# A gated mix of attention and a state-space convolution, rewritten around a list schedule

## The chip, the cores and the metric

The kernel runs on one core of a Trainium2 chip. Its time is the device time of one execution in microseconds (us). Three runs of the kernel before took 1487.04, 1490.69 and 1493.61 us; the median, 1490.69, is what the prediction is compared with. A core has five engines with an instruction stream each, which execute in order and meet at semaphores: PE (matmuls; PEld is its loading of weights), DVE (element-wise work), ACT (exponentials and other functions), POOL, and SP, which here only issues transfers. SBUF is the memory beside the engines; PSUM, with eight banks of 512 f32 columns on 128 partitions, is where matmuls write.

## The reference

```python
x = A_x                                        # 2048 positions x 448 channels, bf16
g = sigmoid((x * gate_w).sum(-1, keepdims=True))
# a: attention, 16 heads of 28, one shared key and value head
q = (x @ wq).reshape(1, 2048, 16, 28).transpose(0, 2, 1, 3); k = x @ wk; v = x @ wv
p = softmax(einsum("bhqd,bkd->bhqk", q, k) * 28 ** -0.5)
a = einsum("bhqk,bkd->bhqd", p, v).transpose(0, 2, 1, 3).reshape(1, 2048, 448) @ wo
# b: each channel d is convolved with its own causal kernel of 2048 lags, 256 complex modes n
logdA = exp(log_dt)[:, None] * (A_re + 1j * A_im); dB = exp(log_dt)[:, None] * (B_re + 1j * B_im)
K = einsum("dn,dnl,dn->dl", C_re + 1j * C_im, exp(logdA[:, :, None] * arange(2048)), dB).real
y = causal_convolution(x, K)                   # written there with FFTs of 4096
b = y + x * Dskip
out = g * a + (1 - g) * b
```

Each mode's power z^l is needed at 2048 lags l = 64 a + b. It is split into a power of z^64 (32 of them, called P, with the factor C dB) and a power of z below 64 (64 of them, Q), so that the kernel of a channel is a product of two small matrices over the modes.

## The kernel before

Everything is written out in an order fixed by hand: a list of instructions for each engine, with a wait wherever a result of another engine (or of DVE itself) is used. Phases follow each other: constants; x loaded and transposed (L297); weights; parameters of the convolution; keys, values and all sixteen query projections (L440), each with a bound on the scores (L452) taken from PSUM by ACT and DVE in turn; the gate; a copy of x by channel, U (L836); then the main phase, and an epilogue after a barrier over all engines.

**Attention, in the main phase.** 512 units go over 4 head groups g, 4 query chunks of 512, 16 key tiles of 128 and 2 pairs of heads. `emit_A` issues the two score matmuls of a unit (L520; 29 rows of the contraction each, so that two heads lie in different quarters of the array) into two of psA's four banks, and the exponential over both on ACT (L527, 1024 columns). `emit_B` issues the two matmuls with the values (L543) into psB0. PE runs two units ahead. At the end of each group of 32 units DVE copies the sums out (L552), PE spreads the row sums (L555), DVE takes the reciprocal of all 128 x 512 (L559) and multiplies (L562).

**The convolution, pumped between the units.** After each unit a step or two of two generators is issued.

- `gen_masters` and `gen_tables`: for a chunk of 16 channels (28 chunks) DVE squares z ten times, 32 columns an instruction (L909 to L926), and doubles the tables Q and P step by step, real and imaginary parts apart (L980 to L1001). Two chunks are interleaved.
- `gen_round`: 112 rounds, one for each group of 4 channels, and at first one for each chunk. A round may transpose the output of the round before (L1047) and copy it to Ysd (L1094), generates the kernels of a chunk (L1064: 64 matmuls of 64 columns; copied out at L1105 and written to the DRAM array KP_scratch by four transfers), and convolves a group (L1082: 17 blocks of 128 lags x 4 channels, 128 columns each; copied out at L1115). Rounds alternate between the banks psC0 and psC1.
- `gen_bts_dma`: the convolution multiplies by a matrix with constant diagonals, BtS, which is read from KP_scratch with rows that overlap: 4 x 2176 elements on each of 128 partitions, 2176 KB a group, two buffers.

All transfers of the main phase stand in SP's queue, in order.

**Epilogue.** 16 blocks of 128 positions: four matmuls with Wo (L642) and five DVE instructions (L653 to L666).

What sets the order is the pump, the same for every unit:

```python
for u in range(n_units):
    emit_unit(u)
    pump(ts, "ts_done", tab_quota)       # table steps: DVE
    if u >= 8:
        pump(rsi, "rs_done", rnd_quota)  # steps of rounds: PE, then DVE
```

## Time and profile before

| | us |
|---|---|
| runs | 1487.04, 1490.69, 1493.61 |
| profiled execution, span | 1487.7 |
| ACT busy, of it exponentials (L527) | 564.8, 518.5 |
| DVE busy | 844.6 |
| PE busy: scores L520, values L543, convolution L1082, kernel generation L1064 | 851.8: 276.0, 284.5, 223.5, 39.0 |
| largest DMA issue: BtS, 112 of 2176 KB, issue to landing (median) | 9.8 |

The profile is that of one execution. A group is the set of instructions of one line, engine and shape; behind the bar stand the group's busy time, the mean length of one in ns, and the idle time of the engine just before them with what ended it. A slice row gives, for 40 equal parts of the span, the busy share in tenths, and PEclk the clock that was granted to PE, in tenths of full speed (where it shows 9 before 222 us it has no record yet). Instructions of one engine may overlap a little, so busy time is less than count times length.

### The profile page before, as it was taken

The page shows a single profiled execution, that of the slowest core. Times are in us where ns is not written, and L with a number is a line of the kernel's source. Part 1 is how long each engine was busy: PE and PEld are TensorE (multiplying, and loading weights), DVE is VectorE, ACT ScalarE, POOL GpSimd, SP SyncE. Part 2 cuts the span into 40 slices and gives each one's busy share as a digit, 9 for nine tenths or more (in the row PEclk, how much of TensorE's full clock was granted, in tenths as well). Part 3 has the DMA queues.
Part 4 walks back from the last instruction along what each step waited for, and adds up shares of the span by engine and source line. Part 5 has one row for each costly group of instructions (what it writes and reads, how often), then busy time and mean ns, then how long its engine had stood idle before and what let it go on. Part 6 is the DMA issues. An engine that isn't in the chain of part 4 may idle for free.

```text
span 1487.7 us, 29922 instructions
## 1 busy us (share of the span) xinstructions
PE 851.8 (57%) x12049; PEld 342.3 (23%) x12049; DVE 844.6 (57%) x4331; ACT 564.8 (38%) x613; POOL 14.7 (1%) x24
## 2 busy tenths in 40 slices
PE   4276195445745467445746366656567665567644
PEld 2022111111212022111212133323233332223311
DVE  1522999999999999999999520200101001010058
ACT  4222084335634455435534333333333333333300
POOL 3000000000000000000000000000000000000000
PEclk9999998556665566656666656565566656665655
DMA  4000002213330233303331489989899898999922
GB/s 98 17 7 0 0 1 65 63 62 125 125 124 21 104 125 125 95 31 124 125 125 60 175 322 353 348 326 361 319 353 334 334 357 306 351 335 338 347 85 65
DMA packets 87355, 261.59 MB, mean 176 GB/s; under 512 B 20496, under 2 KB 29648, under 8 KB 87216
## 3 DMA queue, kind: packets, MB, share of 16 engines
q1 hardware_dynamic: 86464, 258.75, 48.8%
q0 software_dynamic: 752, 0.93, 0.4%
q8 instruction: 94, 1.54, 0.4%
q14 instruction: 45, 0.37, 0.1%
HBM read 255.77 MB, written 3.90 MB: 175 GB/s over the span
## 4 chain that ended last, share of the span: by engine, by line
DVE 47%; DMA 28%; PE 20%; issue 2%; ACT 1%; SPq 0%; DVEq 0%
DMA BtS<-KP_scratch 26%; PE psC L1082 8%; DVE tabQ L987 5%; DVE rden_sb L559 3%; PE psA L520 3%; PE psB L543 3%; DVE tmpT L984 3%; DVE tabQ L980 3%; DVE tabQ L981 3%; DVE U L836 2%; PE psA L440 2%; DVE mst L909 2%; DVE tmpT L983 2%; DVE tabP L994 2%; DVE tabP L993 2%
## 5 line engine op out<-in xcount | busy, mean ns | idle before, releaser
L527 ACT ACTIVATE expT<-psA 128x1024 bf16<-128x1024 f32 x512 | 518.5, 1024 | 760.8 <-PE psA L520 714.3
L1082 PE MATMUL psC<-BtS,U 128*16 128x128 bf16 x7616 | 223.5, 284 | 183.8 <-DMA BtS<-KP_scratch 183.5
L543 PE MATMUL psB<-expT,vaug 128*32 128x512 bf16 x1024 | 284.5, 552 | 48.4 <-DVE rden_sb L559 31.7
L520 PE MATMUL psA<-qT,kT 29*128 29x512 bf16 x1024 | 276.0, 536 | 5.0 <-DVE psC L1163 5.0
L1115 DVE CAST cstg<-psC 128x128 bf16<-128x128 f32 x112 | 32.3, 288 | 429.2 <-PE psC L1082 420.8
L1082 PEld LDWEIGHTS psC<-BtS,U 128*16 128x16 bf16 x7616 | 161.0, 115 | 257.0 <-DMA BtS<-KP_scratch 200.5
L1064 PE MATMUL psC<-tabQ,tabP 128*32 128x64 bf16 x1792 | 39.0, 241 | 159.1 <-DVE tabP L1001 159.1
L520 PEld LDWEIGHTS psA<-qT,kT 29*128 29x128 bf16 x1024 | 51.3, 97 | 212.7 <-issue 207.5
L543 PEld LDWEIGHTS psB<-expT,vaug 128*32 128x32 bf16 x1024 | 61.3, 115 | 148.2 <-ACT expT L527 107.5
L987 DVE TENSOR_TENSOR tabQ<-tabQ,tmpT 128x1024 bf16<-128x1024 bf16 (+2 forms) x168 | 75.8, 488 | 0.0
L1064 PEld LDWEIGHTS psC<-tabQ,tabP 128*32 128x32 bf16 x1792 | 29.5, 120 | 173.1 <-DVE tabP L1001 162.3
L559 DVE RECIPROCAL rden_sb<-psB 128x512 f32<-128x512 f32 x16 | 53.7, 3358 | 9.9 <-PE psB L555 9.9
L1094 DVE COPY Ysd<-psC 128x64 bf16<-128x64 bf16 x112 | 24.8, 222 | 50.1 <-PE psC L1047 50.1
L981 DVE TENSOR_TENSOR tabQ<-tabQ,mbf 128x512 bf16<-128x512 bf16 (+2 forms) x168 | 53.2, 317 | 0.0
L980 DVE TENSOR_TENSOR tabQ<-tabQ,mbf 128x512 bf16<-128x512 bf16 (+2 forms) x168 | 53.2, 317 | 0.0
L984 DVE TENSOR_TENSOR tmpT<-tabQ,mbf 128x512 bf16<-128x512 bf16 (+2 forms) x168 | 53.1, 316 | 0.0
L983 DVE TENSOR_TENSOR tmpT<-tabQ,mbf 128x512 bf16<-128x512 bf16 (+2 forms) x168 | 53.1, 316 | 0.0
L555 PE MATMUL psB<-acc_sb,cbf 128*128 128x512 bf16 x16 | 8.4, 526 | 74.3 <-DVE acc_sb L552 74.3
L909 DVE TENSOR_TENSOR mst<-mst 128x32 f32<-128x32 f32 x280 | 49.7, 178 | 0.0
L910 DVE TENSOR_TENSOR mst<-mst 128x32 f32<-128x32 f32 x280 | 49.7, 177 | 0.0
L1047 PE MATMUL psC<-cbf,cstg 128*128 128x128 bf16 x112 | 29.6, 264 | 35.0 <-DVE cstg L1115 35.0
L924 DVE CAST mbf<-mst 128x32 bf16<-128x32 f32 x280 | 47.0, 168 | 0.0
(123 smaller groups left out, 805.6 us busy)
## 6 DMA issues: line engine op xcount, KB each, us to landing
BtS<-KP_scratch SPq DMA_DIRECT2D x112, 2176.0 KB, 9.8
xstage<-in_A_x_dram SPq DMA_DIRECT2D x16, 112.0 KB, 2.1
KP_scratch<-kstg SPq DMA_DIRECT2D x112, 16.0 KB, 1.9
xs_epi<-in_A_x_dram SPq DMA_DIRECT2D x16, 112.0 KB, 2.0
out_dram<-osb SPq DMA_DIRECT2D x16, 112.0 KB, 1.7
Wo<-in_A_wo_dram POOLq DMA_DIRECT2D x4, 98.0 KB, 2.6
Wq<-in_A_wq_dram POOLq DMA_DIRECT2D x3, 112.0 KB, 4.8
xstage<-in_B_A_re_dram SPq DMA_DIRECT2D x3, 64.0 KB, 3.1
```

The costliest lines, as they stand in the source:

```text
L520: hsc = pg.op("pe", lambda e, hsl=hsl, kt=kt, g=g, qc=qc, slot=slot, hs2=hs2: e.matmul(psA.v(0, P, 1024 * slot + 512 * hs2, [[1, 512]]), k ...
L527: hact = pg.op("act", lambda e, slot=slot, es=es: e.activation(expT.v(0, P, es * 1024, [[1, 1024]]), psA.v(0, P, 1024 * slot, [[1, 1024]]) ...
L543: hpv = pg.op("pe", lambda e, hsl=hsl, kt=kt, es=es, hs2=hs2: e.matmul(psB0.v(32 * hsl, 32, 0, [[1, 512]]), vaug.v(0, P, 32 * kt, [[1, 32] ...
L559: h3 = pg.op("dve", lambda e: e.reciprocal(rden.v(0, P, 0, [[1, 512]]), psB0.v(0, P, 0, [[1, 512]])))
L909: h1 = pg.op("dve", lambda e, nre=nre, a=a: e.tensor_tensor(nre, a, a, ALU.mult))
L980: h1 = pg.op("dve", lambda e: e.tensor_tensor(q_c(0, b_dst, w), q_c(0, b_src, w), m_b(lvl, 0, w), ALU.mult))
L981: h2 = pg.op("dve", lambda e: e.tensor_tensor(q_c(1, b_dst, w), q_c(1, b_src, w), m_b(lvl, 0, w), ALU.mult))
L983: h3 = pg.op("dve", lambda e: e.tensor_tensor(tmp_c(0, w), q_c(1, b_src, w), m_b(lvl, 1, w), ALU.mult))
L984: h4 = pg.op("dve", lambda e: e.tensor_tensor(tmp_c(1, w), q_c(0, b_src, w), m_b(lvl, 2, w), ALU.mult))
L987: h5 = pg.op("dve", lambda e: e.tensor_tensor(q_both(b_dst, w), q_both(b_dst, w), tmp_both(w), ALU.add))
L1064: h_pe_last = pg.op("pe", lambda e, psC=psC, j=j, bl=bl, comp=comp, g8=g8, Q=Q, Pt=Pt, ci=ci: e.matmul(psC.v(32 * j, 32, 256 + 64 * bl, [[ ...
L1082: h_pe_last = pg.op("pe", lambda e, psC=psC, m=m, cg=cg, d=d, BtS=BtS: e.matmul(psC.v(32 * cg, 16, 0, [[1, 128]]), U.v(0, P, d * 32 + 16 - ...
```

## The change

The kernel is written anew. What it computes is the same; the parts are these.

1. **Order.** Operations are recorded with what they read and write, an estimated duration and a priority, and a list scheduler fixes the order of every engine before the program runs. There are no phases and no barrier: the prologue, attention, convolution and output are one graph.
2. **Exponentials over three banks.** Score tiles go three at a time (L849) into one half of a six-bank psS, and ACT takes 1536 columns (L859). The value matmuls (L874) are three at a time too, into one bank, psB.
3. **Projections in the loop.** Query projections and their bounds (L600 to L610) are computed one group ahead, in the eighth bank, psX, instead of in a prologue.
4. **Normalisation.** The gate is multiplied in (L823); the four rows of sums are gathered by transfers into 128 x 16, the reciprocal is taken there (L828), and the result is spread by way of DRAM.
5. **Power tables.** P and Q of 16 channels, real and imaginary, are neighbours in one tile and doubled together: five levels of three DVE instructions with 128 to 2048 columns (L685, L688, L693) and a last one for the upper 32 powers of Q (L701 to L708). The masters are squared for four chunks at once (L645 to L657).
6. **Convolution.** The 128 rows of the contraction are two halves of 64 lags, 1024 lags apart; the matrix T of a group has 1024 elements for each channel and partition (four buffers, two transfers of 512 KB), and a group is 16 blocks x 4 channels of 64 columns (L763). Results go through DRAM (Y_scratch) to a layout by channel.
7. **One bank for four uses.** Projection, kernel generation (L724), convolution and output (L804) hold psX in turn, by a lock in the schedule; each holds it until DVE has copied it out.
8. **Output.** Mixing with the gate is done in place in xT (L786, L788) and added on PE by a matmul with the identity (L807).

The core of the diff:

```diff
-    def phase_main(self):                     # and gen_masters, gen_tables, gen_round, attn_units
...
+    def schedule(self):                       # takes the operation that can start first, then by priority
+            for e in ENG:
+                T = free[e]
+                for i in ready[e]:
+                    r = max(rt[i], T)
+                    if o.lock is not None:
+                        if L[0] is not None:
+                            continue
+                        r = max(r, L[1])
+                    key = (r, o.pr, i)
+                    if best is None or key < best[0]:
+                        best = (key, e, i)
...
+    def tables(self, c):
+        for lv in range(5):
+            w = 1 << lv
+            pg.op("dve", lambda e, d=dst3, a=src, m=m, w=w: e.tensor_tensor(
+                d, a, mbf.v(0, P, m, [[HC, 4], [0, w], [1, HC]]), ALU.mult),
+                el(n, 1.92), rd=rk + mk, wr=[("tab", s, lv + 1)], pr=pr)
+            pg.op("dve", lambda e, a=src, m=m, w=w: e.tensor_tensor(
+                tmp.v(0, P, so, [[w * HC, 4], [HC, w], [1, HC]]), a, mbf.v(0, P, m + 128, [[HC, 4], [0, w], [1, HC]]), ALU.mult),
+                el(n, 1.92), rd=rk + mk, wr=[("tmp", s)], pr=pr)
+            pg.op("dve", lambda e, d=d2, t=t2: e.tensor_tensor(d, d, t, ALU.add), el(n, 1.92),
+                  rd=[("tmp", s), ("tab", s, lv + 1)], wr=[("tab", s, lv + 1)], pr=pr)
...
+    def tload(self, gi):
+        pg.dma([(self.T.v(64 * h, 64, s * 4096, [[1024, 4], [1, 1024]]),
+                 dram(self.KP, d0 * KPW + 1024 * h, [[1, 64], [KPW, 4], [1, 1024]])) for h in range(2)],
+               128 * 8192, f"T{s}", rd=[("KP", c), "pad"], wr=[("T", s)], pr=1)
...
+    def conv(self, c, u):
+        for k in range(2):
+            for m in range(0, 16, 2):
+                    for mm_ in (m, m + 1):
+                        for j in range(4):
+                            r = e.matmul(self.psX.v(32 * j, 32, 64 * k, [[1, 64]]),
+                                         self.U.v(0, P, uo + (15 - mm_) * DT + d, [[DT, 32]]),
+                                         self.T.v(0, P, s * 4096 + j * 1024 + 960 - 64 * mm_, [[1, 64]]),
+                                         start=(mm_ == 0), stop=(mm_ == 15), tile_position=(0, 32 * j), skip_group_check=True)
+        pg.op("dve", lambda e: e.tensor_copy(self.cst.v(0, P, cs * 256 + 128 * u, [[64, 2], [1, 64]]),
+                                             self.psX.v(0, P, 63, [[64, 2], [-1, 64]])),
+              el(128), rd=[X], wr=[("cst", cs)], pr=2, unlock="X")
...
+        def qk(b):
+                for k, (qc, g, kt, h) in enumerate(ts):
+                    r = e.matmul(self.psS.v(0, P, 1536 * s + 512 * k, [[1, 512]]),
+                                 kT.v(32 * h, DH + 1, 128 * kt, [[1, 128]]),
+                                 qT.v(32 * h, DH + 1, 512 * qs, [[1, 512]]),
+                                 start=True, stop=True, tile_position=(32 * h, 0), skip_group_check=True)
...
+            pg.op("act", lambda e: e.activation(expT.v(0, P, 1536 * es, [[1, n]]), self.psS.v(0, P, 1536 * s, [[1, n]]),
+                                                AF.Exp, scale=SQ), 185 + n / 1.2, rd=bk, wr=[("e", es)], pr=0)
```

How the rows of an engine move, at three places. On PE in the convolution's stage the kernel before has, with psA and psB0 for scores and values, psC for the convolution (L1082) and its transpose (L1047):

```order
L543 MATMUL psB<-expT,vaug 32x512 x2
L520 MATMUL psA<-qT,kT 128x512 x2
L1082 MATMUL psC<-BtS,U 16x128 x20
L543 MATMUL psB<-expT,vaug 32x512 x2
L520 MATMUL psA<-qT,kT 128x512 x2
L1047 MATMUL psC<-cbf,cstg 128x128
L1082 MATMUL psC<-BtS,U 16x128 x36
```

and the change, in the middle of its stream:

```order
L849 MATMUL psS<-qT,kT 128x512 x3
L874 MATMUL psB<-expT,vaug 32x512 x3
L763 MATMUL psX<-T,U 32x64 x40
L849 MATMUL psS<-qT,kT 128x512 x3
L874 MATMUL psB<-expT,vaug 32x512 x3
L763 MATMUL psX<-T,U 32x64 x24
```

Pairs become triples, the transposes are gone, and pieces of the convolution stand behind the triples through most of the stream and not in its second part alone. On DVE, in the middle, the kernel before has the tables (tabQ, tmpT) and masters (mst, mbf) of two chunks interleaved:

```order
L983 TENSOR_TENSOR tmpT<-tabQ,mbf 128x64
L984 TENSOR_TENSOR tmpT<-tabQ,mbf 128x64
L924 CAST mbf<-mst 128x32
L925 TENSOR_SCALAR mbf<-mst 128x32
L926 TENSOR_SCALAR mbf<-mst 128x32
L924 CAST mbf<-mst 128x32
```

and the change (cst is what the convolution is copied to, acc what the values are):

```order
L648 TENSOR_TENSOR mst<-msq 128x128
L693 TENSOR_TENSOR tab<-tab,tmp 128x4x128
L651 SCALAR_TENSOR_TENSOR mst<-mst 128x128
L770 CAST cst<-psX 128x128
L685 TENSOR_TENSOR tab<-tab,mbf 128x4x256
L823 TENSOR_TENSOR acc<-psB,grow 128x512
L688 TENSOR_TENSOR tmp<-tab,mbf 128x1024
L606 TENSOR_REDUCE absq<-psX 128x512
L693 TENSOR_TENSOR tab<-tab,tmp 128x4x256
```

DVE has 1142 rows where it had some 3940, longer ones, and the copies out of psX and psB stand between products of up to 2048 columns. On SP, of the kernel before, where the matrices are loaded once the last chunks are written:

```order
L120 DMA BtS<-KP_scratch 128x4x2176
L120 DMA KP_scratch<-kstg 32x4x64 x4
L120 DMA BtS<-KP_scratch 128x4x2176
L120 DMA KP_scratch<-kstg 32x4x64 x4
L120 DMA BtS<-KP_scratch 128x4x2176 x86
```

and of the change, where denT, R_scratch and rdenB are the steps of a normalisation and Y_scratch is the output of the convolution:

```order
L95 DMA denT<-acc 32x1x16 x4
L95 DMA T<-KP_scratch 64x4x1024 x4
L95 DMA Y_scratch<-cst 32x4x64 x4
L95 DMA R_scratch<-denT 128x16
L95 DMA KP_scratch<-kstg 32x4x64 x4
L95 DMA rdenB<-R_scratch 32x512 x4
L95 DMA T<-KP_scratch 64x4x1024 x8
```

SP now issues some 640 transfers in the place of some 300; the loads of T stand among the steps of the normalisation and the writes of both scratch arrays.

1918 lines of the change are left out of this document (792 added, 1126 removed).

## The prediction

> **What bounds the kernel now.** I read the page first, then the waits, then the same stretches engine by engine. From the page: the span, busy time, four of the slice rows (40 slices of 37 us) and the chain of work by engine.
>
> ```profile
> span 1487.7 us, 29922 instructions
> PE 851.8 (57%) x12049; PEld 342.3 (23%) x12049; DVE 844.6 (57%) x4331; ACT 564.8 (38%) x613; POOL 14.7 (1%) x24
> DVE  1522999999999999999999520200101001010058
> ACT  4222084335634455435534333333333333333300
> PEclk9999998556665566656666656565566656665655
> DMA  4000002213330233303331489989899898999922
> DVE 47%; DMA 28%; PE 20%; issue 2%; ACT 1%; SPq 0%; DVEq 0%
> ```
>
> No engine is busy for 60% of the span, yet DVE is full from slice 5 to 21 and DMA from slice 24 to 38: two stages, one after the other, each with one limit, while the exponentials of ACT trickle through both. The waits say who suffers (us in total, times, longest):
>
> ```profile
> ACT expT L527 <- PE psA L520: 714.3, 361, 18.2
> PE psC L1064 <- DVE tabP L1001: 159.1, 14, 17.1
> PE psC L1082 <- DMA BtS<-KP_scratch: 183.5, 70, 7.7
> ```
>
> PE executes in order. When a kernel-generation matmul (L1064) waits up to 17 us for a table, or a convolution (L1082) up to 7.7 us for its matrix, the scores (L520) behind it wait too, and ACT starves: 714 us. Four stretches (us; busy and count on PE, PEld, DVE, ACT, POOL; clock; DMA share; GB/s):
>
> ```profile
> 148.00:185.00 37.00, 5.96 (x52) 4.09 (x52) 36.66 (x25) 0.41 (x1) 0.00 (x0) 1.00 0.00 0
> 185.00:222.00 37.00, 35.12 (x126) 6.47 (x126) 36.99 (x278) 33.31 (x33) 0.00 (x0) 1.00 0.00 1
> 703.00:740.00 37.00, 27.48 (x354) 9.30 (x354) 34.79 (x185) 21.09 (x21) 0.00 (x0) 0.64 0.39 126
> 888.00:925.00 37.00, 24.39 (x444) 12.04 (x443) 3.10 (x12) 14.11 (x14) 0.00 (x0) 0.64 0.95 353
> ```
>
> The first exponential runs only after 185 us of prologue. Then 33 exponentials fit into 37 us; in the table stage 21, in the DMA stage 14. So the three resources are used in turn, and a kernel that uses them together has the largest of their sums for a floor, not the total. I work these sums out for the new kernel.
>
> **ACT.** 1024 score tiles of 512 columns go three to an instruction: 341 of 1536 columns and one of 512, in place of 512 of 1024.
>
> ```profile
> L527 ACT ACTIVATE expT<-psA 128x1024 bf16<-128x1024 f32 x512 | 518.5, 1024 | 760.8 <-PE psA L520 714.3 <-DVE mst L913 41.0
> L447 ACT ACTIVATE qT<-psA 128x512 bf16<-128x512 f32 x16 | 9.6, 597 | 39.1 <-PE psA L440 39.1
> ```
>
> 512 more columns cost 1024 - 597 = 427 ns, so 1536 columns cost 1.45 us, and all exponentials 341 x 1.45 + 0.6 = 495 us (518 before). That is the cadence which the others must keep: 1.45 us an exponential.
>
> **DVE.** Groups by form, then two successive instructions of the timeline (start, length):
>
> ```profile
> L987 DVE TENSOR_TENSOR tabQ<-tabQ,tmpT 128x1024 bf16<-128x1024 bf16 x84 | 53.6, 675 | 0.0
> L980 DVE TENSOR_TENSOR tabQ<-tabQ,mbf 128x512 bf16<-128x512 bf16 x84 | 34.3, 408 | 0.0
> L987 DVE TENSOR_TENSOR tabQ<-tabQ,tmpT 128x256 bf16<-128x256 bf16 x28 | 6.7, 280 | 0.0
> L987 DVE TENSOR_TENSOR tabQ<-tabQ,tmpT 128x128 bf16<-128x128 bf16 x28 | 5.0, 216 | 0.0
> L909 DVE TENSOR_TENSOR mst<-mst 128x32 f32<-128x32 f32 x280 | 49.7, 178 | 0.0
> L924 DVE CAST mbf<-mst 128x32 bf16<-128x32 f32 x280 | 47.0, 168 | 0.0
> L562 DVE TENSOR_TENSOR onT<-acc_sb,rden_sb 128x512 bf16<-128x512 bf16 x16 | 11.1, 691 | 0.6
> L1105 DVE CAST kstg<-psC 128x256 bf16<-128x256 f32 x28 | 11.7, 417 | 13.6 <-PE psC L1082 13.4
> L1115 DVE CAST cstg<-psC 128x128 bf16<-128x128 f32 x112 | 32.3, 288 | 429.2 <-PE psC L1082 420.8 <-PE psB L543 8.4
> 701.49 0.41 DVE L993 TENSOR_TENSOR tabP<-tabP,mbf 128x512 bf16<-128x512 bf16 x1
> 701.82 0.41 DVE L994 TENSOR_TENSOR tabP<-tabP,mbf 128x512 bf16<-128x512 bf16 x1
> ```
>
> A bf16 product costs 675 - 408 = 267 ns per 512 columns, so 2048 columns cost 675 + 2 x 267 = 1209 ns (extrapolated; no row has that size). A chunk of 16 channels now takes three instructions at each of 128, 256, 512, 1024, 2048 and once more 2048 columns: 3 x (0.22 + 0.28 + 0.41 + 0.68 + 1.21 + 1.21) = 12.0 us, and 0.17 for a seed copy; 28 chunks: 341 us. Elements in f32 cost (691 - 178) / 480 = 1.07 ns a column, so the doubling masters, now 7 batches of 128 columns, take per level 0.42 (256 columns) + 0.28 + 0.28 + 0.35 (a cast of 256: between L924's 0.17 and L1105's 0.42, nearer the larger, as the size is) + 0.42 = 1.75; ten levels and a first, seven times: 128 us, where L909, L910, L913, L916 and L924 to L926 now take some 320. Evacuations: 28 x 0.42 + 56 x 0.29 = 28; query projections 16 x 1.4 = 22; normalisation 16 x 1.6 = 26 (its reciprocal now has 16 columns, 0.25 us by the 3.36 us of 512); mixing and output 28. Sum 573. Successive independent instructions start 0.33 us apart at 0.41 us length, so up to 75 ns of each of the 1100 may vanish; in the new order a sum follows its two products at once, so I take half: 573 - 41 = 532, ends 490 and 573. In the table stage today DVE is busy for 34.79 of 37 us (94%); with that share 532 take 566 us. **This is the largest of the sums, and I take it as the bound**, 14% above ACT's.
>
> **PE.** Convolution: 7168 matmuls of 64 columns in place of 7616 of 128 (lags split into two halves stacked on the partitions). Three matmuls of scores and of values at a time instead of two. In the timeline at 706 us the clock is low, at 708.5 high:
>
> ```profile
> 705.58 0.95 PE L1064 MATMUL psC<-tabQ,tabP 128*32 128x64 bf16 x48 [15.56 <-DVE tabP L1001]
> 706.34 0.62 PE L543 MATMUL psB<-expT,vaug 128*32 128x512 bf16 x2
> 706.89 0.61 PE L520 MATMUL psA<-qT,kT 29*128 29x512 bf16 x2
> 708.50 0.39 PE L543 MATMUL psB<-expT,vaug 128*32 128x512 bf16 x2
> 708.82 0.39 PE L520 MATMUL psA<-qT,kT 29*128 29x512 bf16 x2
> 709.14 0.62 PE L1082 MATMUL psC<-BtS,U 128*16 128x128 bf16 x32
> 197.54 0.61 PE L520 MATMUL psA<-qT,kT 29*128 29x512 bf16 x2
> 80.21 1.94 PE psA L440 x4
> ```
>
> Start to start, a pair takes 0.55 us at the low clock and 0.32 at the high one, no longer than one matmul, since its two lie in different quarters of the array. The third lies in another quarter again, so I price a triple like a pair (upper end: 1.5 times). Kernel generation takes 0.76 / 48 = 15.8 ns a matmul of 64 columns, the form that the convolution now has. So 341 x 1.1 + 8960 x 0.0158 + 16 projections at 2.5 (four matmuls 1.94 at 80.21, and the bound 0.6) = 375 + 142 + 40 = 557 us at the low clock, and 218 + 142 + 21 = 381 at the high one. Which clock? From 185 to 222 us PE is busy 35.12 of 37 us with pairs alone, and each is still 0.61 long, as the row at 197.54 shows: attention alone does not raise it. The granted clock rises in trace rows only where convolution and kernel generation run densely beside it (708.5). The new order has 8 to 48 convolution or kernel-generation matmuls behind three of four pairs of triples, so I expect the clock mostly high and PE below DVE.
>
> [...]
>
> **DMA.** The matrices of the convolution shrink from 2176 to 1024 KB a group, with as many packets (112 x 512), now of 2 KB.
>
> ```profile
> BtS<-KP_scratch SPq DMA_DIRECT2D x112, 2176.0 KB, 9.8
> KP_scratch<-kstg SPq DMA_DIRECT2D x112, 16.0 KB, 1.9
> 1443.00:1480.00 37.00, 20.05 (x48) 5.14 (x48) 34.23 (x59) 0.00 (x0) 0.00 (x0) 0.50 0.24 69
> L642 PE MATMUL psA<-Wo,onT 128*128 128x448 bf16 x64 | 26.6, 574 | 26.7 <-DVE d L658 22.4 <-DVE Ysd L1094 4.3
> ```
>
> From 888 us, 353 GB/s at share 0.95 are 187 ns of an engine per packet of 4352 B; from 1443 us, 69 GB/s at 0.24 in packets of 896 B are 50 ns. Between them 2 KB costs 96 ns: 57344 x 96 / 16 = 344 us, against 670 at the old price (upper end) and 315 by bytes alone. The chunk's 128 B rows written for the output (28 times 64 KB, new) come on top like those of KP_scratch. 344 lies well below DVE. What hides it is the prefetch into four buffers; gone, it costs its landing, below.
>
> **Head and tail.** Before the first exponential DVE has in its new order some 29 us of work (ten products of 896 columns at 1.1, four copies of 1024, five reductions and small things), behind some 8 us of load and transposes: 38 to 40 us in place of 185 (30 to 55). After the last exponential: value matmul 0.6, product 0.7, three transfers of 1.9, 0.25 and 0.7 are 8 us; then seven output tiles, each 20 matmuls of 112 columns (20 x 112 / 448 x 26.6 / 64 = 2.1) and an evacuation of 0.6 with its hand-over 0.3, one after another in one bank: 21; the store 2. 31 us.
>
> **Sum.** 40 + 566 + 31 = 637 us of span. The profiled execution has 1487.7 and the median of the runs is 1490.69, 3 above: **640 us**.
>
> **Rivals.**
> 1. *ACT becomes the bound*, and DVE's instructions overlap like today's best: 40 + 495 + 31 + 3 = **570**. For it: DVE's lower end, 490. Against: nothing then may ever hold ACT.
> 2. *One bank, psX, is handed round.* Kernel generation (28), convolution (56) and projections (16) each hold it until DVE has copied it out, and PE, in order, waits with the scores behind it. Price: half of a 1.2 us product in front, 0.3 to 0.7 for the copy, two hops: 1.3 us; 100 of them unhidden give 130: **770**. For it: today's 714 us of ACT behind PE are of this kind. Against: two exponentials' worth of scores lie ahead in six banks, so a wait under 1.45 us need not reach ACT.
> 3. *The clock stays low*: 557 us of PE at, say, 90%: 40 + 619 + 31 + 3 = **690**. For it: the PEclk row today (5 and 6). Against: today PE idles for 7 to 17 us at a time, which the denser stream should not.
> 4. *Slower than before: SP serialises the loads.* Every load, and the small transfers of the normalisation, stand in one queue in order. If each of the 112 groups waits for its buffer, then for a landing as long as today's 9.8 us, then convolves for 3, this is 12.8 us a group: 40 + 1434 + 31 + 3 = **1508**. It is slower than before from 12.6 us a group. Against: half the bytes, four buffers, and the DMA slices today show two loads under way at once (6.3 us a group at 353 GB/s).
>
> **How the numbers follow.** The forecast 0.57, rival 1 0.10, rival 2 0.18, rival 3 0.12, rival 4 0.03. The likeliest gives 640. The range must leave out no more than 0.2: from 570 (rival 1) to 790 (rival 2 with part of the cold clock); what lies above is rival 4 and mixtures. Bounds inside the forecast: DVE 490 to 573, idle share 2 to 10%, head 30 to 55, that is 565 to 725. The three runs spread by 0.4%, so 0.5% is what can be told from no change. Faster 0.96, within 0.5% 0.01, slower 0.03 (rival 4).
>
> **What would show it.** DVE busy in nine tenths of the slices from the first exponential to the last table, 530 to 575 us; ACT near 495; first exponential at 40 us; PEclk at 8 or more. Rival 1: DVE gaps, ACT full. Rival 2: waits of PE on L734, L770 or L610 in the hundreds, one to two us each. Rival 3: triples of 0.61 us throughout. Rival 4: convolution waiting for T, some 10 us each time. The forecast is wrong above all if product times at 2048 columns leave the line drawn through 512 and 1024, or if the order fixed in advance makes engines wait in turn, which no sum shows.

## The result, and the profile after

| | us |
|---|---|
| before, median (4 runs) | 1490.83 (1487.04 to 1493.61) |
| after, median (4 runs) | 844.68 (843.82 to 846.69) |
| ratio after / before, 95% interval | 0.567 (0.5656 to 0.5684) |
| forecast, its range | 640 (570 to 790) |

The change is faster by 43%. The forecast had the direction, but the time lies 205 us above it and 55 us above the range. The page of the changed kernel: span, busy times, five slice rows (40 slices of 21 us), the largest DMA queue and the chain of work.

```profile
span 843.0 us, 25548 instructions
PE 556.3 (66%) x11601; PEld 323.5 (38%) x11616; DVE 525.7 (62%) x1153; ACT 495.8 (59%) x362; POOL 30.1 (4%) x43
DVE  4999776676576765685576656884667765501311
ACT  3358667574576756575666656774466764838600
PEclk9655667666686768686667776886687786958755
DMA  9500885998939989988999699888996899999211
GB/s 188 83 1 1 178 176 115 181 203 173 216 74 215 198 160 221 219 175 160 222 189 203 123 222 225 174 173 176 216 217 139 177 219 224 187 219 192 55 30 28
q1 hardware_dynamic: 128974, 134.84, 79.1%
DMA 33%; PE 28%; DVE 17%; issue 10%; SPq 9%; POOL 2%; ACT 1%; ACTq 0%; POOLq 0%
```

The sums of the three compute engines came out near what was reckoned: ACT 495.8 us (495 forecast), DVE 525.7 (532), PE 556.3 (557 at the low clock, by chance, as is shown under PE below). What differs is the row that was to stand far below them: DMA shows 8 or 9 in most slices from the fifth to the 37th, and DVE, which was to be full, mostly 5 to 7. Three stretches, the main one, the end of the exponentials and the tail (columns as in the prediction's stretches):

```profile
80.00:740.00 660.00, 451.30 (x10245) 264.41 (x10258) 442.85 (x984) 415.75 (x296) 0.00 (x0) 0.73 0.91 184
740.00:780.00 40.00, 27.98 (x730) 18.31 (x727) 3.90 (x9) 25.38 (x19) 0.00 (x0) 0.72 1.01 204
800.00:843.00 43.00, 14.34 (x140) 12.68 (x140) 5.92 (x10) 0.00 (x0) 0.00 (x0) 0.54 0.12 28
```

The first and the last exponentials in ACT's timeline:

```profile
46.83 1.45 ACT L859 ACTIVATE expT<-psS 128x1536 bf16<-128x1536 f32 x1 [8.32 <-PE psS L849]
796.45 1.94 ACT L859 ACTIVATE expT<-psS 128x1536 bf16<-128x1536 f32 x2 [1.10 <-PE psS L849]
```

From 80 to 780 us the 16 DMA engines are busy for nine tenths or more, at 184 to 204 GB/s. Before, a share of 0.95 moved 353 GB/s. So the DMA engines are full, but at little more than half the rate. The waits (us in total, times, longest):

```profile
ACT expT L859 <- PE psS L849: 267.9, 152, 10.5
PE psX L763 <- issue: 76.1, 29, 5.6
PE psX L763 <- DMA T<-KP_scratch: 31.3, 17, 5.1
PE psX L763 <- DVE kstg L734: 21.5, 6, 6.6
PE psX L763 <- DVE cst L770: 20.4, 6, 10.5
```

The DMA issues (count, size, us from issue to landing):

```profile
T<-KP_scratch SPq DMA_DIRECT2D x224, 512.0 KB, 10.7
KP_scratch<-kstg SPq DMA_DIRECT2D x112, 16.0 KB, 7.6
Y_scratch<-cst SPq DMA_DIRECT2D x112, 16.0 KB, 9.9
```

A load of 512 KB takes longer to land than one of 2176 KB did before (10.7 us against 9.8), and the writes of KP_scratch, which stand behind loads in the one queue, take 7.6 us against 1.9.

The price of a packet can be counted in the trace, packet by packet. This table holds before, after and the experiments on the price further below. Before has 57,344 packets of 4352 B; every other row has 59,392 of 2 KB (57,344 of T, the rest of rdenB). "Of 16 engines" is the sum of their times divided by 16.

| kernel | packet, bytes | mean ns | median ns | of 16 engines, us |
|---|---|---|---|---|
| before (128 rows) | 4352 | 191 | 168 | 684 |
| after | 2048 | 156.1 | 162 | 579 |
| 128 rows, two packets at a time | 2048 | 87.8 | 85 | 326 |
| paired rows | 2048 | 102.6 | 84 | 381 |
| paired rows, lower half first | 2048 | 122.1 | 84 | 453 |
| one channel a load | 2048 | 113.6 | 84 | 422 |
| far rows, 64 | 2048 | 151.7 | 160 | 563 |
| far rows, 128 | 2048 | 95.0 | 84 | 353 |
| pitch 2303 | 2048 | 156.5 | 161 | 581 |
| even and odd rows | 2048 | 98.9 | 84 | 367 |

The prediction had reckoned 96 ns and 344 us.

### The profile page after: what moved, and what is told of

Its sections match the earlier page's. It is cut to its first block, busy times and chain, and to the rows that moved or that the text cites. A ratio compares the mean times of both kernels' runs of the same rounds, so it can differ in the third digit from the quotient of the medians.

```text
span 843.0 us, 25548 instructions
## 1 busy us (share of the span) xinstructions
PE 556.3 (66%) x11601; PEld 323.5 (38%) x11616; DVE 525.7 (62%) x1153; ACT 495.8 (59%) x362; POOL 30.1 (4%) x43
## 3 DMA queue, kind: packets, MB, share of 16 engines
q1 hardware_dynamic: 128974, 134.84, 79.1%
## 4 chain that ended last, share of the span: by engine, by line
DMA 33%; PE 28%; DVE 17%; issue 10%; SPq 9%; POOL 2%; ACT 1%; ACTq 0%; POOLq 0%
DMA T<-KP_scratch 9%; DMA denT<-acc 9%; SPq L95 9%; PE psX L763 8%; PE psS L849 7%; DMA R_scratch<-denT 5%; PE psB L874 4%; DMA rdenB<-R_scratch 4%; PE psX L724 4%; PE psX L804 2%; DMA yT<-Y_scratch 2%; DVE tmp L688 2%; DMA out_dram<-osb 2%; DVE tab L693 2%; DVE tab L685 2%
## 5 line engine op out<-in xcount | busy, mean ns | idle before, releaser
L859 ACT ACTIVATE expT<-psS 128x1536 bf16<-128x1536 f32 x342 | 479.7, 1452 | 279.2 <-PE psS L849 267.9
L763 PE MATMUL psX<-T,U 128*32 128x64 bf16 x7168 | 198.4, 239 | 155.6 <-issue 76.1
L763 PEld LDWEIGHTS psX<-T,U 128*32 128x32 bf16 x7168 | 161.8, 155 | 184.1 <-issue 81.0
L849 PE MATMUL psS<-qT,kT 29*128 29x512 bf16 x1024 | 172.8, 497 | 34.7 <-issue 13.6
L874 PE MATMUL psB<-expT,vaug 128*32 128x512 bf16 x1024 | 173.2, 497 | 12.1 <-DVE acc L823 6.8
L724 PE MATMUL psX<-tab 128*32 128x64 bf16 x1792 | 80.8, 301 | 26.7 <-issue 10.8
L770 DVE CAST cst<-psX 128x128 bf16<-128x128 f32 x56 | 16.0, 286 | 120.0 <-PE psX L763 116.3
L874 PEld LDWEIGHTS psB<-expT,vaug 128*32 128x32 bf16 x1024 | 35.2, 97 | 129.0 <-issue 116.5
L685 DVE TENSOR_TENSOR tab<-tab,mbf 128x2048 bf16<-128x2048 bf16 (+4 forms) x140 | 78.6, 565 | 0.4
L688 DVE TENSOR_TENSOR tmp<-tab,mbf 128x128 bf16<-128x128 bf16 (+4 forms) x140 | 78.5, 563 | 0.0
L693 DVE TENSOR_TENSOR tab<-tab,tmp 128x128 bf16<-128x128 bf16 (+4 forms) x140 | 77.8, 563 | 0.4
L724 PEld LDWEIGHTS psX<-tab 128*32 128x32 bf16 x1792 | 60.9, 144 | 35.6 <-issue 14.1
L849 PEld LDWEIGHTS psS<-qT,kT 29*128 29x128 bf16 x1024 | 34.6, 95 | 73.4 <-issue 35.4
L804 PE MATMUL psX<-Wo,onT 128*128 128x112 bf16 x256 | 28.6, 282 | 33.2 <-DMA out_dram<-osb 19.1
L828 DVE RECIPROCAL denT<-denT 128x16 f32<-128x16 f32 x16 | 4.0, 252 | 62.1 <-DMA denT<-acc 62.1
L804 PEld LDWEIGHTS psX<-Wo,onT 128*128 128x128 bf16 x256 | 23.7, 136 | 37.8 <-DMA out_dram<-osb 21.5
L701 DVE TENSOR_TENSOR tab<-tab,mbf 128x2048 bf16<-128x2048 bf16 x28 | 34.1, 1218 | 0.0
L708 DVE TENSOR_TENSOR tab<-tab,tmp 128x2048 bf16<-128x2048 bf16 x28 | 34.0, 1215 | 0.0
L657 DVE TENSOR_TENSOR mbf<-mst,sgn 128x256 bf16<-128x256 f32 x70 | 29.1, 416 | 0.0
## 6 DMA issues: line engine op xcount, KB each, us to landing
T<-KP_scratch SPq DMA_DIRECT2D x224, 512.0 KB, 10.7
```

The lines of the kernel that those rows point to most:

```text
L685: pg.op("dve", lambda e, d=dst3, a=src, m=m, w=w: e.tensor_tensor(d, a, mbf.v(0, P, m, [[HC, 4], [0, w], [1, HC]]), ALU.mult), el(n, 1.92) ...
L688: pg.op("dve", lambda e, a=src, m=m, w=w: e.tensor_tensor(tmp.v(0, P, so, [[w * HC, 4], [HC, w], [1, HC]]), a, mbf.v(0, P, m + 128, [[HC, ...
L693: pg.op("dve", lambda e, d=d2, t=t2: e.tensor_tensor(d, d, t, ALU.add), el(n, 1.92), rd=[("tmp", s), ("tab", s, lv + 1)], wr=[("tab", s, l ...
L701: pg.op("dve", lambda e: e.tensor_tensor(dst, src, mbf.v(0, P, m, [[HC, 2], [0, 32], [1, HC]]), ALU.mult), el(n, 1.92), rd=rk + mk, wr=[(" ...
L724: r = e.matmul(self.psX.v(32 * j, 32, 64 * g, [[1, 64]]), tab.v(0, P, to + (4 + comp) * BLK + o, [[HC, 32]]), tab.v(0, P, to + comp * BLK ...
L763: r = e.matmul(self.psX.v(32 * j, 32, 64 * k, [[1, 64]]), self.U.v(0, P, uo + (15 - mm_) * DT + d, [[DT, 32]]), self.T.v(0, P, s * 4096 + ...
```

## Experiments: is it the loads?

A time with a range behind it is the median of four runs; a time without one is a single run. The four runs of one kernel lie within 2% of each other.

**T loaded once.** Loads of T only for the first four groups; the convolution then works on what lies in the buffers.

```diff
     def tload(self, gi):
         pg = self.pg
+        if gi >= self.NTR:
+            return
```

> The matrices T are loaded for the first four groups only; the 108 later groups convolve with what lies in the buffers (so the convolution's output is not the reference's). All other work and the rules of the schedule stay. Theory A (the transfers are the bound: the loads of T take 59392 packets of 2 KB at 156 ns over 16 engines, 579 of 843 us, and everything small queues behind them): DMA share falls under 0.2, landings of the small transfers fall from 4 to 10 us to about 2, and the time falls to 620 to 690, what the sum of DVE gave. Rival B (the bank psX handed round, PE in order): the hand-overs are all still there, time stays above 780. Rival C (the small transfers of the normalisation hold DVE, whatever the queue): above 750.

Measured: 669.01 us, in A's range and below its rivals'. The main stretch of this run:

```profile
80.00:560.00 480.00, 397.61 (x10589) 252.89 (x10591) 432.64 (x980) 398.65 (x288) 0.00 (x0) 0.91 0.17 32
```

and the landing of KP_scratch among its issues:

```profile
KP_scratch<-kstg SPq DMA_DIRECT2D x112, 16.0 KB, 1.6
```

Without the loads DVE is busy for 90% of the main stretch (432.64 / 480; with them 442.85 / 660, 67%), the clock goes from 0.73 to 0.91, a small write lands in 1.6 us again, and 176 of the 205 us are gone. This is the work of the loads and of the order together: the scheduler leaves the loads out of its reckoning too, and DVE's order differs from its 219th instruction on. The run with even and odd rows, further below, keeps the order and makes the loads cheap: 148 us are gone there, and the clock rises from 0.72 to 0.82. So the loads are the cause of most of the miss, and the low clock followed from them.

**Normalisation without its transfers.** The chain of waits of the changed kernel, by line:

```profile
DMA T<-KP_scratch 9%; DMA denT<-acc 9%; SPq L95 9%; PE psX L763 8%; PE psS L849 7%; DMA R_scratch<-denT 5%; PE psB L874 4%; DMA rdenB<-R_scratch 4%; PE psX L724 4%; PE psX L804 2%; DMA yT<-Y_scratch 2%; DVE tmp L688 2%; DMA out_dram<-osb 2%; DVE tab L693 2%; DVE tab L685 2%
```

The normalisation's three transfers (denT, R_scratch, rdenB) stand there with 18% of the span, twice as much as the loads of T. Here they are removed, and the 16 reciprocals between them; rdenB is set to 1.

```diff
-        pg.dma([... self.denT ... acc ...])        # gather the sums
-        pg.op("dve", lambda e: e.reciprocal(dv, dv), ...)
-        pg.dma([(dram(self.R, i * 2048, ...), dv)], ...)
-        pg.dma([(self.rdenB.v(...), dram(self.R, ...))], ...)
+        # once, on POOL: rdenB = 1.0
```

> The normalisation leaves out its gathering, reciprocal, DRAM round trip and spreading: rdenB is set to one once (so the attention is not divided by its sums). 144 small transfers go, and DVE no longer waits for them. Theory A: DVE's 98 us of waits on denT and rdenB go, but the loads of T stay the bound: 800 to 840. Rival C: 740 to 770 (the 98 us come off whole).

Measured: 838.63 us, 6 less: A's range, not C's. A chain names who came last at each step, not what the time would be without him: with the loads as the limit, other waits take over, and PE's waits for T at the convolution grow from 31.3 to 52.9 us. The order moved here too (DVE's from its 155th instruction on), so the 6 us are not the price of these transfers alone.

**The planner told 205 GB/s.** The scheduler that fixes the order holds a transfer rate; only it is changed, and with it the order.

```diff
-    DMA_BW = 330.0
+    DMA_BW = 205.0
```

> One number of the schedule's own price list is changed: transfers at 205 B/ns where it had 330, close to what the trace of the change shows during the loads (about 200 GB/s). The work is the same, only the order moves. Theory A (transfers are the bound): 820 to 850, since no order moves them faster. Rival C (engines wait in turn because the order was made for faster transfers): the waits of DVE on denT and rdenB (98 us) and of PE on T fall to less than half, and the time to 740 to 790.

Measured: 783.03 us, 62 less, with nearly the same price of a packet (151.9 ns). That is C's range and not A's. Of C's two signs one came: DVE's waits on denT and rdenB fall from 98 to 8.4 us, but PE's waits for T at the convolution, which were to halve, double from 31.3 to 65.3. An order made for cheap loads costs something by itself when they are dear, beside the loads and not in their place.

## Experiments: why does a packet cost 156 ns?

**One load of 128 rows a channel.** The two halves of T (rows 0 to 63 and 64 to 127) in one transfer.

```diff
-        pg.dma([(self.T.v(64 * h, 64, s * 4096, [[1024, 4], [1, 1024]]),
-                 dram(self.KP, d0 * KPW + 1024 * h, [[1, 64], [KPW, 4], [1, 1024]])) for h in range(2)],
+        pg.dma([(self.T.v(0, P, s * 4096 + 1024 * j, [[1, 1024]]),
+                 dram(self.KP, (d0 + j) * KPW, [[1024, 2], [1, 64], [1, 1024]])) for j in range(4)],
```

> Same bytes, same number of packets of 2 KB, but each transfer of T fills 128 partitions with one channel (four transfers of 256 KB a group) where it filled 64 partitions with four channels (two of 512 KB). [...] Theory A2 (a packet of this overlapping read costs some 160 ns whatever its form): packets and time as in the change, 830 to 860. Rivals B and C: time within 2% of 845.

Measured: 2650.0 us (2649.73 to 2650.81), 1.78 times the kernel before (1.773 to 1.785). The chain of this run by engine:

```profile
SPq 69%; DMA 17%; PE 7%; DVE 4%; issue 1%; POOL 1%; ACT 0%; ACTq 0%; POOLq 0%
```

and a row of SP's timeline (start, length, seven issues in a row):

```profile
1003.89 31.12 SPq L95 DMA_DIRECT2D T<-KP_scratch  x7
```

Each of these loads holds SP for 4.4 us (31.12 / 7). By the trace two packets of 2 KB are in flight for 2144 of the 2648 us, and the queue's packets fill 15.2% of the 16 engines' span. The source's outermost dimension is 2 here, and two packets at a time are nearly the whole run (57,344 x 88 ns / 2 = 2520 us). So A2 missed the time, and so did theory A1, which holds the writing to one half of the partitions for the cause and had 690 to 760 us; but the run gives the price of a packet beside one other, 85 ns in the median, and with it the question why a packet needs 162 in the changed kernel, where 16 or more of 2 KB are in flight for 461 of the 843 us.

**Paired rows.** Theory A1 was that all engines write to the same half of the partitions. Row 2m + h of T, in the place of 64h + m, holds half h; U's rows likewise. One load goes to all 128 rows with 64 as the outer dimension. PE, DVE, ACT and SP keep their order.

```diff
+        pg.dma([(self.T.v(0, P, s * 4096 + 1024 * j, [[1, 1024]]),
+                 dram(self.KP, (d0 + j) * KPW, [[1, 64], [1024, 2], [1, 1024]])) for j in range(4)],
```

> The same 59,392 packets of 2 KB, the same bytes and the same order of work on TensorE, VectorE, ScalarE and SP; only the rows of T are laid out otherwise: row 2m+h holds lag 64-block m of half h (before: row 64h+m), so that one load goes to 128 rows, its 16 engines write to both halves of the partitions at once, and the outer dimension of its source is 64 (not 2, as in the run on 128 rows that took 2650 us with two packets in flight at a time). U's rows are permuted alike. Each group of four channels has four loads of 256 KB where it had two of 512 KB. Theory A1 (a packet of 2 KB costs 156 ns in the changed kernel because all 16 engines write to the same 64 partitions, where the two engines at a time of the 128-row run needed 88 ns): mean packet of 85 to 105 ns, the T loads 315 to 390 us of 16 engines, the DMA share 50 to 60%, and a time of 640 to 730 us. Rival A2 (some 210 GB/s is what 16 engines get from these overlapping rows of one small stretch of memory, whichever partitions they write): packets stay at 145 to 165 ns and the time at 820 to 860 us.

Measured: 735.19 us (728.98 to 743.21). The ratio to before, 0.4923 (0.4893 to 0.4953), is that of the three runs up to 737.54. Packets cost 102.6 ns in the run of 743 us. The price is A1's; the time lies 5 us above its 730. Its issues land sooner:

```profile
T<-KP_scratch SPq DMA_DIRECT2D x448, 256.0 KB, 4.8
KP_scratch<-kstg SPq DMA_DIRECT2D x112, 16.0 KB, 2.6
```

**Half of T by POOL's queue.** Rows as in the changed kernel.

```diff
+        for h, q in ((0, "sp"), (1, "pool")):
+            pg.dma([(self.T.v(64 * h, 64, ...), dram(self.KP, d0 * KPW + 1024 * h, ...))], ..., eng=q)
```

> T's rows as in the changed kernel, but the half h=1 is loaded by POOL's queue and h=0 by SP's, so that two queues are in flight and, when both are, the engines write to both halves of the partitions. The order that the planner makes changes somewhat, since the loads are two operations now. Theory A1 (both halves at once is what the packets need): mean packet of 90 to 130 ns, time 680 to 780 us. Rival A2 (a ceiling of some 210 GB/s by the source): packets 145 to 170 ns, time 800 to 860 us. Rival A3 (the small transfers suffer by standing behind T in one queue, and half of T on another queue relieves them): packets as in the changed kernel, KP_scratch landing in under 5 us instead of 7.6, time 760 to 820 us.

Measured: 809.73 us; SP's 2 KB packets 146 ns, POOL's came as packets of 4 KB at 269. The packets miss A1's 90 to 130, and the time lies in the ranges of A2 and A3 both; no run shows whether packets to both halves were in flight together. KP_scratch lands in 3.9 us, as A3 says. With an order that differs somewhat, 35 us are not enough to say for what.

**Paired rows, the lower half first**, and **one channel a load** with the rows of the changed kernel: both write to one half of the partitions at a time, in eight loads of 128 KB a group.

```diff
+        pg.dma([(self.T.v(64 * q, 64, s * 4096 + 1024 * j, [[1, 1024]]),
+                 dram(self.KP, (d0 + j) * KPW + 32 * q, [[1, 32], [1024, 2], [1, 1024]])) for q in range(2) for j in range(4)],
```
```diff
+        pg.dma([(self.T.v(64 * h, 64, s * 4096 + 1024 * j, [[1, 1024]]),
+                 dram(self.KP, (d0 + j) * KPW + 1024 * h, [[1, 64], [1, 1024]])) for h in range(2) for j in range(4)],
```

> Rows of T, rows of U, sources and order of work as in the run with paired rows (735 us, packets of 102.6 ns), and every load again of one channel; only each load of 128 rows is cut into one of rows 0 to 63 and one of rows 64 to 127, the four lower ones first. So the 16 engines write to one half of the partitions at a time, as in the changed kernel, while the source is read as in the paired run. Theory A1 (writing to both halves at once is what made the packets cheap): packets back to 140 to 160 ns, time 810 to 880 us. Rival A2b (the interleaved source rows made them cheap): packets stay at 95 to 110 ns; the time is then 735 to 790 us, since SP now issues eight loads a group instead of four, at about 0.5 us each, 224 us more for SP.

> The changed kernel's rows of T (64h+m), with loads of one channel and one half each: eight of 128 KB a group, 64 rows of 2 KB from one stretch of 2.2 KB. Same order. Against the run with halves (median 84 ns) only this differs: a load reads one stretch of 2.2 KB, not two 2 KB apart in turn. Theory H: 140 to 165 ns in the median, 950 to 1050 us (SP issues 896 loads, as there, 997 us). Rival W and rival K: the median at 84 to 95 ns, since a load has one piece a row and no pitch, 950 to 1010 us.

Measured: 996.89 and 991.78 us, means of 122.1 and 113.6 ns, medians of 84 in both. The first misses the ranges of A1 and of its rival alike; the second lies in those of W and K. The medians seemed to speak against A1. The chain of the first, by engine, shows why they don't:

```profile
SPq 45%; PE 19%; DMA 17%; DVE 14%; issue 4%; POOL 2%; ACT 0%; POOLq 0%
```

and its main stretch:

```profile
80.00:740.00 660.00, 385.55 (x8483) 215.35 (x8477) 374.39 (x863) 348.57 (x248) 0.00 (x0) 0.66 0.59 152
```

SP, with 896 loads to issue, leads the chain with 45%, and the stretch moves 152 GB/s, below the 184 to 204 of the changed kernel (the second run moves 152 there too). The expectation of the run with far rows, the next, still reads these medians as a doubt of A1; that was wrong, since a price measured at 152 GB/s is no evidence on the price at 184 to 204.

**Far rows.** T read from 64 rows of x that lie 2046 B apart, and **a pitch of 2303** elements in the scratch: two rivals on the source's side.

```diff
-                 dram(self.KP, d0 * KPW + 1024 * h, [[1, 64], [KPW, 4], [1, 1024]])) for h in range(2)],
+                 dram(self.ins["A_x"], 65536 * ((2 * gi + h) % 11), [[1023, 64], [65536, 4], [1, 1024]])) for h in range(2)],
-KPW = 2112
+KPW = 2303
```

> The changed kernel's loads of T as they are (two a group, rows 64h+m, four channels a row, the same order), but read from the input x instead: 64 rows that lie 2046 B apart and hardly overlap, where they lie 2 B apart in the scratch (so 64 rows of a channel are one stretch of 2.2 KB). The convolution then has other data: the output is not the reference's, the work the same. The run with halves has put theory A1 (all engines write to one half) in doubt: there the median packet was 84 ns although each load went to one half. Theory H (16 engines that read one stretch of 2.2 KB of memory at the same time get some 210 GB/s): 84 to 100 ns a packet, 700 to 770 us. Rival W (the way that these loads write T, 64 rows and four pieces a row, is what is slow): 145 to 165 ns, 825 to 860 us. Rival K (the pitch of 4224 B between a row's four pieces in the scratch): 84 to 100 ns here too.

> The changed kernel with one number changed: a channel's row in the scratch is 2303 elements long (4606 B, as in the kernel before) instead of 2112 (4224 B). Same order, same loads. Rival K (the pitch): 84 to 105 ns a packet, 700 to 770 us. Theory H and rival W: 145 to 165 ns, 825 to 860 us.

Measured: 838.5 us and 151.7 ns; 846.02 us and 156.5 ns. Neither the overlap of the rows nor the pitch explains the price. Theories H and K fall, and what is left is the side that is written: 64 neighbouring rows, or four pieces a row.

**Far rows to 128 rows, four pieces each**, and **even and odd rows**: paired rows with the changed kernel's two loads a group, one to the 64 even rows, one to the 64 odd ones.

```diff
+        pg.dma([(self.T.v(0, P, s * 4096, [[1024, 4], [1, 1024]]),
+                 dram(self.ins["A_x"], 65536 * (gi % 6), [[1023, 128], [131072, 4], [1, 1024]]))],
```
```diff
+        pg.dma([(bass.AP(tensor=self.T.h, offset=h * self.T.rs + s * 4096, ap=[[2 * self.T.rs, 64], [1024, 4], [1, 1024]]),
                  dram(self.KP, d0 * KPW + 1024 * h, [[1, 64], [KPW, 4], [1, 1024]])) for h in range(2)],
```

> Far rows of the input x as in the run before (838 us, 152 ns a packet), but one load of 1 MB a group to all 128 rows, four pieces of 2 KB a row, instead of two loads of 64 rows. The output is not the reference's, since T holds other data; order and bytes are the same. Theory A1 (the drain into 64 neighbouring rows is the limit, some 210 GB/s): 84 to 100 ns a packet and 680 to 760 us. Rival W4 (four pieces a row are the limit): 145 to 165 ns, 820 to 860 us.

> Paired rows of T and U (row 2m+h), but the changed kernel's two loads a group: the first writes the 64 even rows, the second the 64 odd ones, four pieces a row, sources and order as in the changed kernel. Theory A1 in its form with neighbouring rows (what limits is the lower or upper half of the partitions): 84 to 100 ns a packet and 690 to 740 us, no more than the 735 us of the paired run, since SP issues half as many loads. A1 in its form with a number of rows (64 rows at a time, wherever they lie), and rival W4: 145 to 165 ns, 820 to 860 us.

Measured: 683.48 us and 95.0 ns; 696.9 us (694.92 to 701.12), 98.9 ns, ratio to before 0.4685 (0.4666 to 0.4703). Both lie in A1's ranges. The page of even and odd rows, where PE, DVE, ACT and SP have the order of the changed kernel:

```profile
span 694.7 us, 25561 instructions
GB/s 203 126 1 0 8 245 264 80 252 266 294 152 220 183 182 325 271 226 236 294 230 293 177 299 244 225 236 210 320 143 269 197 286 212 306 262 112 50 20 27
q1 hardware_dynamic: 128974, 134.84, 63.3%
T<-KP_scratch SPq DMA_DIRECT2D x224, 512.0 KB, 6.6
```

and one of its waits:

```profile
PE psX L764 <- issue: 32.7, 22, 3.8
```

The same packets, pieces, sources, sizes and number of loads; only the destination's rows (and U's with them) lie two apart, not one. So it is neither the four pieces nor the number of rows, but that they are neighbours in one half. No run separates the two halves of that: 64 neighbouring rows from the middle, half of them below row 64 and half above, were not tried. The price of the neighbouring rows comes with time: counted from a pause in the loads (0.2 us without a new packet), the changed kernel's packets have a median of 84 ns from the 33rd to the 96th, 95 to the 128th, 165 to the 192nd and 161 after the 1024th; with even and odd rows it stays at 84. What makes it rise, no run shows. By the mean packet, 64 neighbouring rows take 16 x 2048 B / 156.1 ns = 210 GB/s and every other row 16 x 2048 B / 98.9 ns = 331; the fullest slice of the one page shows 225 GB/s, that of the other 325.

## Experiments: what does the order cost?

With the rows mended, the planner got prices nearer to the traces: 450 ns of SP for an issue (60 before; the trace of the changed kernel has medians of 350 to 591 ns for the small transfers and 617 for a load of T), and other rates and latencies. The issue's price and the rate were changed together, so no run says which of them counts for how much.

```diff
-                free[e] = r + 60.0 * o.ndma
+                free[e] = r + 450.0 * o.ndma
```

Paired rows, 300 GB/s and 2 us; then 230 GB/s and 2.5 us:

> The paired rows (735 us) with a planner that is told what was measured: 450 ns of SP for an issue instead of 60, and 300 GB/s instead of 330. Nothing that runs is changed but the order. Theory O (of the 66 us that the paired run lies above the 669 us without loads, a good part is an order made for transfers that start and land earlier than they do): 680 to 715 us. Rival P (the rest is the transfers themselves, 381 us of 16 engines in bursts, and SP's 16% on the chain, whatever the order): 725 to 750 us.

> As the run before it, with 230 GB/s and 2.5 us of latency in the planner: the order is made for slower transfers than were measured, so that loads are asked for earlier and the work behind them later. Theory O: 680 to 720 us, about as with 300 GB/s. If the order is over-cautious: kernel generation and convolution bunch toward the end, ACT is done early and a stretch of convolution alone is left, 720 to 760 us. Rival P: 725 to 750 us.

Measured: 705.22 us (702.84 to 709.44), ratio 0.475 (0.4732 to 0.4768), and 691.82 (689.94 to 694.43), ratio 0.4652 (0.4637 to 0.4666), against 735: both in theory O's ranges. In the second the exponentials run out in the stretch from 560 us, and convolution alone waits for its loads, as its expectation feared, yet the whole costs less. Two stretches of it:

```profile
560.00:600.00 40.00, 19.98 (x610) 13.70 (x604) 6.29 (x13) 12.86 (x10) 0.00 (x0) 0.64 0.86 261
600.00:640.00 40.00, 18.26 (x704) 16.15 (x697) 6.29 (x13) 0.00 (x0) 0.00 (x0) 0.50 0.92 286
```

Even and odd rows, with 230 GB/s and 2.5 us; with 300 and 2 us, in one run and then in four; and with 360 and 1.5 us:

> The run with even and odd rows, with the planner's prices of the 692 us run (450 ns of SP an issue, 230 GB/s, 2.5 us). If packets are cheap there: 665 to 700 us, with VectorE busy in nine tenths of the slices up to the last table. If they are not (A1 by number of rows, W4): 760 to 800 us, as the changed kernel's rows had with 205 GB/s in the planner (783).

> The same with 300 GB/s and 2 us in the planner (705 us with four loads a group). If packets are cheap: 670 to 710 us; if not: 780 to 840 us.

> The kernel of the 669 us run (even and odd rows; planner with 450 ns of SP an issue, 300 GB/s, 2 us), timed for an interval: 664 to 675 us, against 697 of the same rows with the order of the changed kernel.

> The same rows, planned for 360 GB/s and 1.5 us. If the rest of the gap to the forecast is the order's, nearer to what the packets can do: 645 to 665 us. If it is VectorE's share, head and tail (VectorE 522 us at 0.92 of the time, 40 us before the first exponential, some 90 us after the last table): 664 to 685 us.

| planner | us | ratio to before, 95% |
|---|---|---|
| as in the change (60 ns, 330, 2 us) | 696.9 | 0.4685 (0.4666 to 0.4703) |
| 450 ns, 230, 2.5 us | 680.3 (677.34 to 682.47) | 0.4563 (0.4546 to 0.458) |
| 450 ns, 300, 2 us | 669.36; then 665.47 (659.98 to 668.48) | 0.4463 (0.4436 to 0.4489) |
| 450 ns, 360, 1.5 us | 727.15 (723.27 to 733.08) | 0.4883 (0.4848 to 0.4919) |

The best is 179 us under the changed kernel. The runs with 230 and 300 GB/s came out as expected, within a microsecond. The last one missed both of its ranges: a plan with 20% more rate and half a microsecond less latency costs 62 us, while the packets cost the same (97.9 ns). Its chain:

```profile
DMA 34%; DVE 28%; PE 20%; SPq 12%; issue 3%; POOL 2%; ACT 0%; POOLq 0%
```

Transfers and SP lead it again. That the order asks for loads too late is a reading of this chain; no run of its own shows it. The page of the best one:

```profile
span 664.0 us, 25565 instructions
DVE  2999999899999998998888899897998986111411
DMA  8900078766947779678859596887897699985211
DVE 42%; PE 32%; DMA 11%; issue 6%; ACT 5%; SPq 3%
```

its first wait:

```profile
ACT expT L860 <- PE psS L850: 87.3, 94, 3.5
```

two stretches:

```profile
80.00:560.00 480.00, 394.09 (x9836) 245.72 (x9846) 434.98 (x975) 401.54 (x291) 0.00 (x0) 0.90 0.78 244
560.00:600.00 40.00, 31.46 (x844) 20.35 (x837) 5.68 (x13) 32.33 (x24) 0.00 (x0) 0.87 0.91 277
```

and the first and the last exponentials of its timeline:

```profile
49.30 2.79 ACT L860 ACTIVATE expT<-psS 128x1536 bf16<-128x1536 f32 x2
611.00 4.62 ACT L860 ACTIVATE expT<-psS 128x1536 bf16<-128x1536 f32 x4
```

DVE is now what the forecast had made it: busy for 8 or 9 tenths up to the last table, and at the head of the chain. ACT's waits for scores fall from 267.9 to 87.3 us.

## Why the prediction was wrong

**The step that failed is the price of a packet** in the part on DMA: "Between them 2 KB costs 96 ns: 57344 x 96 / 16 = 344 us". Measured are 156 ns and 579 us, rdenB's packets included (560 for the 57344 of T). The interpolation ran over packet sizes alone. But the row at its upper end (4352 B, 128 rows a load) wrote to all partitions, and the change, described in front as two loads to 64 rows each, does not. 96 ns is near what was measured where rows of both halves are written: 95.0 and 98.9. The sentence "344 lies well below DVE" is where DMA should have been found to be the bound.

**The price alone is not the whole miss.** With 579 us for DMA the prediction's own sum would still give 40 + 579 + 31 + 3 = 653. By the trace, three more things bring it to 845. The small transfers, which the prediction says "come on top" and gives no time, raise the queue's work from 579 to 667 us (79.1% of 843). The loads cannot start with the first exponential: the first is issued at 86.6 us, the last at 769. And in the stretch from 80 to 780 us the share of DMA is 0.92, not 1. So 80 us ahead of this stretch, the 700 us in it and 63 us behind it are the 843 of the span; for head and tail together the prediction had 71.

**A rival was missing.** The text kept an upper end of 670 us for the loads, but did not carry it through the sum: 40 + 670 + 31 + 3 = 744 as a case of its own, "the loads become the bound". No rival was of this kind; rival 4 has loads one after another, which did not happen (751.6 us from first to last exponential are 6.7 us for each of 112 groups, where it had 12.8).

**The caveat on the order** ("the order fixed in advance makes engines wait in turn, which no sum shows") held, and was given no time. It is at least 31 us with cheap packets (696.9 to 665.5) and 62 us with dear ones (844.7 to 783.0, one run).

Of the 205 us, measured one after another: rows 148 (844.7 to 696.9), order 31 (to 665.5), and 25 that stay.

Point by point:

- *ACT.* 495 us; measured 495.8, an exponential 1.45 us. Right.
- *DVE.* 532 us; measured 525.7. The products of 2048 columns, extrapolated to 1209 ns, are 1215 to 1218. The bound itself was hidden by the loads. In the best kernel the stretch from the first to the last exponential is 615.6 - 49.3 = 566.3 us, where 532 / 0.94 = 566 was forecast. That they agree so well is partly luck: DVE is busy for 91% of the main stretch, not 94%, has little left after 560 us, and 24 exponentials of the next 40 us, and some more, still follow.
- *PE.* The low-clock sum, 557, equals the 556.3 measured, but that is chance: the granted clock was 0.72, and the terms missed on both sides. Convolution and kernel generation were busy for 198.4 + 80.8 = 279 us where 142 was reckoned, from one row, for both clocks; scores and values for 172.8 + 173.2 = 346 where 375 was (groups overlap, so they add up to more than the total). So the high-clock sum, 381, is too small. Without the loads, at a clock of 0.91 in the main stretch, 1024 score matmuls take 149.9 us: 0.44 us a triple, where the pair's price of 0.32 was taken. The upper end (1.5 times) holds it. The group of the scores in the run with T loaded once (busy us, mean ns):

```profile
L851 PE MATMUL psS<-qT,kT 29*128 29x512 bf16 x1024 | 149.9, 432 | 10.3 <-ACT expT L861 8.6
```

- *Head and tail.* First exponential at 46.8 us (40 forecast, 30 to 55 as bounds), 44.6 us after the last one (31). In the best kernel 49.3 and 48.4: 27 us above the 71 forecast, which are the 25 us that stay, within 2.
- *Rival 1* (ACT the bound, 570): no; its lower end for DVE, 490, was not reached. *Rival 2* (one bank handed round, 770): its time is the nearest to the result, by luck, since its mechanism is small: PE's convolution waits 21.5 and 20.4 us for the copies at L734 and L770, not hundreds. *Rival 3* (the clock stays low, 690): the clock did stay at 0.73, but as a consequence: without the loads it is 0.91 (both in the main stretch). Over the whole span it was 0.72 here and 0.85 in the best kernel.

## What to carry to other kernels

The price of a packet belongs to where it is written as much as to its size (2 KB took 156 ns to 64 neighbouring rows, 98.9 to every other row): take it from a row whose destination has the same rows, and lay out a tile that is loaded in parts so that each part goes to rows all over the partitions (every other row, not one half). Carry both ends of every bound through the whole sum; an end that passes the forecast bound is a rival of its own. An order fixed in advance depends on its prices, and not evenly: 230, 300 and 360 GB/s gave 680, 665 and 727 us. Feed measured prices back, for issues too, time several orders, and expect tens of us either way. When a sum gives the bound to another engine, ask anew when that engine's work can start and what is left after it: the head and tail are its own.

## What was not expected of the hardware

- By the mean packet, 16 engines that write to 64 neighbouring partitions get 210 GB/s (156 ns for 2 KB), those that write to every other partition 331 (98.9 ns). The 33rd to the 96th packet after a pause still go at 84 ns in the median, those after the 1024th at 161.
- Source rows that overlap almost wholly cost about as much as far ones (156.1 and 151.7 ns).
- A transfer of 128 rows whose source has 2 as its outer dimension had two packets in flight at a time for 2144 of 2648 us and made the kernel 3.1 times as long as the changed one.
- PE's waits that the profile puts down to nothing ("issue", 76.1 us at the convolution) fall to 32.7 us with cheap packets and to at most 8.5 us without the loads (46.6 us of idle time there, 38.1 of them behind DVE's copies). What PE waits for in them, no run shows.
